# A product in four one-bank PSUM buffers from a common pool, a first attention in groups, and a new order of work

## The chip, the core and the metric

The program runs on one core of a Trainium2 chip. The metric is device time in microseconds (us) of one execution. Before the change three timed runs gave 225.18, 226.84 and 223.76 us, median 225.18. The profile is of one more execution of the same program, which took 223.1 us.

The core has five engines that run side by side, each strictly in its own order: TensorE (PE, matrix products; PEld is the loading of its stationary operand), VectorE (DVE), ScalarE (ACT), GpSimd (POOL) and SyncE (SP), which here issues all DMAs. PE writes its products to PSUM, which these kernels use as eight banks of 512 floats in each of 128 partitions; here DVE and ACT read it, and POOL works on SBUF alone.

## What is computed

```python
# x: 4 batches x 12480 tokens x 128 channels, inducing: 32 x 128, all float32
def mab(q, kv):
    s = scale * (q @ kv.transpose(0, 2, 1))       # scale = 1 / sqrt(128)
    s = s - s.max(-1, keepdims=True)
    a = np.exp(s)
    a /= a.sum(-1, keepdims=True) + 1e-09
    return a @ kv
h = mab(I, x)              # first attention: 32 inducing points look at all tokens of a batch
y = mab(x, h)              # second attention: each token looks at the 32 points
u = y @ w_in               # 128 -> 2048, 49920 tokens in all
out = (u - np.tanh(u)) @ w_out                    # 2048 -> 128
```

## The kernel before, in words

**The algebra.** Every row of `y` is a mean of the 32 rows of `h`. The kernel replaces `u - tanh(u)` by its tangent at the mean of `h`, so the last two products shrink to one small matrix per batch, `P` (32 x 128, with a column of ones). Per token there remain scores against `h`, an exponential and one product with `P`, divided by the sum of the exponentials. `bound` works out whether the tangent is close enough and writes `limit`; a general branch behind it is taken only if not.

**The stages.** Each batch has eight full steps of 1536 tokens and a rest step of 192, nine in all.

- `first(b)`: for each step a load of `xT` (channels on partitions, 768 KB), four matmuls of scores (L341 with `indT_sb`), and on DVE a copy out of PSUM with the maxima (L375). After all nine steps the maximum over the batch goes through PE twice (L384, L392) and becomes the bias `nb` (L394). Then for each step an exponential on ACT (L429), a transpose on DVE (L433) and twelve accumulating matmuls into one bank, `hacc` (L440). These need the tokens on partitions as well: for the steps in `TURNED` PE transposes `xT` (L415, three groups of four) and ACT or DVE moves the result to SBUF (L419); for the others a second copy is loaded (`xn`, L423). Then the sums, the division (L456) and a fold (L458) give `h` (`hT_all`, L460).
- `linear(b)`: `h` through `w_in`, tangent, `w_out`: a chain over PE, ACT, DVE and POOL (L475 to L538), at whose end stands `P_all` of the batch.
- `second(b, s)`: scores (L341 with `hT_all`), the maximum on DVE (L559, L560), the exponential on ACT (L563), and the product with `P` on PE (L570), twelve matmuls into `o_ps`, **one tile of four PSUM banks**, bank `q` for a quarter of the tokens. Then DVE adds a small number to the sums in all four banks at once (L582) and inverts them (L583). The eviction is in three pieces: banks 0 and 1 together, bank 2, bank 3. A piece goes either through DVE, which multiplies on the way out (L604), or through ACT as a plain copy (L608) followed by the multiplication on POOL (L612). Then the store (L619).
- `weight`: the weights come as 64-bit words and are turned into floats on ACT, POOL and DVE (L300 to L323) early in the program.

**The order.** The five engines' orders aren't the text's. `Plan.order` goes through a plan of all operations with a cost each, and whenever an engine is free in that plan it takes the ready operation with the least priority number (`pri`, from the table `K`), if the buffers it needs are free. `STAY` is added to operations that would change PE's kind of tile; `TURNED` says which steps are turned on PE. `PLACES` has the number of buffers of each kind (23 large ones, `big`, for loads and results; four one-bank PSUM buffers `ps` beside `o_ps`), `MOST` limits how many serve one purpose. On the chip each engine then waits by semaphores for what its next instruction needs. The semaphores follow the tiles: where DVE and ACT read the same PSUM tile, the later one in the order waits for the earlier.

## Time and profile before

| | |
|---|---|
| median of three timed runs | 225.18 us |
| the profiled execution's own time | 223.1 us |
| its span, first to last instruction | 221.2 us |
| mean granted PE clock | 0.92 of full |
| busy PE / DVE / ACT / POOL | 165.5 / 154.6 / 106.1 / 92.7 us |
| DMA | 67.23 MB, 304 GB/s over the span |

The profile is one execution. Busy time is the time in which an engine executed something; PE's is modelled, as matmuls overlap. A row of the grouped view has line, engine, operation, tiles and shapes, count, then busy us and mean ns of one, then the idle time just before and what ended it (`<-`). A row of the timeline has the start, the duration and the instruction, merged where the same one repeats.

### The profile page before, as it was taken

To read this page: it belongs to the slowest core of one execution; us is meant where nothing else is said; L and a number is where in the kernel's file an instruction comes from. 1 tells how busy PE (TensorE), PEld (TensorE's weight loads), DVE (VectorE), ACT (ScalarE), POOL (GpSimd) and SP (SyncE) were. 2 spreads that over 40 slices of the span, in tenths; PEclk is the share of its full clock that TensorE was granted. 3 is DMA by queue.
4 is the path that set the end of the run, shared out by engine and by line. 5 is a ranking of instruction groups with operands and counts; after the bars stand their busy time and mean duration, and the time that the engine had idled before them with its cause. 6 is when DMAs were issued, how large, how long until landed. Compare 5 with 4: busy or idle time off the path is not lost.

```text
span 221.2 us, 6573 instructions
## 1 busy us (share of the span) xinstructions
PE 165.5 (75%) x2627; PEld 104.2 (47%) x2627; DVE 154.6 (70%) x456; ACT 106.1 (48%) x226; POOL 92.7 (42%) x103
## 2 busy tenths in 40 slices
PE   0999939878599979599986997999787676364320
PEld 0565727433476635255764544667544433133210
DVE  3367889999957657767984778897656957555350
ACT  2122898436377634447942551696445233443200
POOL 4001189766513437563021563304636734436230
PEclk9999999999589999979999999999999859998555
DMA  6999969999649999997999999999956440655640
GB/s 190 419 423 379 400 221 331 413 424 419 217 142 280 366 393 397 340 387 234 304 391 422 383 410 341 417 407 324 395 217 247 184 162 1 284 215 214 257 190 16
DMA packets 13909, 67.23 MB, mean 304 GB/s; under 512 B 1712, under 2 KB 2864, under 8 KB 13872
## 3 DMA queue, kind: packets, MB, share of 16 engines
q1 hardware_dynamic: 13872, 66.74, 79.0%
q8 instruction: 23, 0.38, 0.7%
q14 instruction: 14, 0.11, 0.2%
HBM read 41.17 MB, written 25.56 MB: 302 GB/s over the span
## 4 chain that ended last, share of the span: by engine, by line
PE 33%; DVE 30%; DMA 14%; ACT 13%; issue 5%; POOL 1%; SPq 0%; DVEq 0%; ACTq 0%
PE ps L341 9%; PE o_ps L570 9%; PE ps L415 9%; ACT big L608 8%; DVE big L604 6%; DMA big<-in_xT 6%; DMA big<-in_xn 5%; PE ps L440 3%; DMA out<-big 3%; DVE mb L559 2%; DVE big L317 2%; DVE s L375 2%; DVE big L306 2%; DVE et L433 2%; ACT ex L563 2%
## 5 line engine op out<-in xcount | busy, mean ns | idle before, releaser
L612 POOL TENSOR_TENSOR big<-big,mb 128x768 f32<-128x768 f32 (+1 forms) x49 | 58.4, 1208 | 76.7 <-ACT big L608 67.3
L570 PE MATMUL o_ps<-P_all,ex 32*128 32x129 f32 (+1 forms) x784 | 34.6, 302 | 22.8 <-DVE big L604 13.2
L608 ACT COPY big<-o_ps 128x768 f32<-128x768 f32 (+1 forms) x49 | 32.5, 668 | 29.0 <-DVE S_all L582 14.5
L570 PEld LDWEIGHTS o_ps<-P_all,ex 32*128 32x128 f32 (+1 forms) x784 | 27.5, 198 | 38.6 <-issue 18.9
L415 PE MATMUL ps<-ident,big 128*128 128x128 f32 x216 | 34.3, 303 | 5.0 <-DVE s L375 3.7
L604 DVE TENSOR_TENSOR big<-o_ps,mb 128x384 f32<-128x384 f32 (+1 forms) x47 | 26.0, 577 | 16.5 <-ACT big L608 16.5
L563 ACT ACTIVATE ex<-ps,mb 128x384 f32<-128x384 f32 (+1 forms) x36 | 20.0, 555 | 36.6 <-DVE mb L560 22.9
L341 PE MATMUL ps<-big,indT_sb 128*32 128x384 f32 x256 | 29.6, 527 | 9.4 <-DMA big<-in_xT 8.6
L419 ACT COPY big<-ps 128x512 f32<-128x512 f32 x33 | 19.0, 585 | 34.3 <-PE ps L415 33.6
L415 PEld LDWEIGHTS ps<-ident,big 128*128 128x128 f32 x216 | 26.3, 154 | 17.1 <-issue 4.9
L440 PE MATMUL ps<-big,et 128*32 128x128 f32 x768 | 27.8, 275 | 5.8 <-DVE et L433 4.4
L341 PE MATMUL ps<-big,hT_all 128*32 128x384 f32 x256 | 28.6, 508 | 2.3 <-DVE W L517 1.7
L440 PEld LDWEIGHTS ps<-big,et 128*32 128x32 f32 x768 | 20.8, 109 | 12.6 <-DVE et L433 6.0
L375 DVE TENSOR_SCALAR_CACHE_REDUCE s<-ps 128x384 f32<-128x384 f32 (+1 forms) x36 | 18.2, 509 | 11.2 <-PE ps L341 11.1
L559 DVE TENSOR_REDUCE mb<-ps 128x1 f32<-128x384 f32 (+1 forms) x36 | 18.3, 509 | 4.2 <-PE ps L341 4.1
L429 ACT ACTIVATE s<-s,nb 128x384 f32<-128x384 f32 (+1 forms) x36 | 20.8, 585 | 0.3 <-DVE nb L394 0.3
L433 DVE STREAM_TRANSPOSE et<-s 128x384 f32<-128x384 f32 (+1 forms) x36 | 18.3, 524 | 1.8 <-PE ps L440 1.2
L419 DVE COPY big<-ps 128x512 f32<-128x512 f32 x21 | 14.2, 686 | 4.2 <-PE ps L415 4.0
L582 DVE TENSOR_SCALAR S_all<-o_ps 128x12 f32<-128x12 f32 (+1 forms) x36 | 5.8, 162 | 14.3 <-PE o_ps L570 13.3
L300 POOL TENSOR_SCALAR big<-big 128x512 f32<-128x512 f32 x8 | 6.4, 809 | 19.3 <-DMA big<-in_w_in 19.3
L341 PEld LDWEIGHTS ps<-big,indT_sb 128*32 128x32 f32 x256 | 6.5, 112 | 16.4 <-issue 11.1
L341 PEld LDWEIGHTS ps<-big,hT_all 128*32 128x32 f32 x256 | 6.9, 110 | 8.8 <-issue 4.3
(115 smaller groups left out, 173.2 us busy)
## 6 DMA issues: line engine op xcount, KB each, us to landing
big<-in_xT SPq DMA_DIRECT2D x32, 768.0 KB, 8.6
out<-big SPq DMA_DIRECT2D x32, 768.0 KB, 5.2
big<-in_xn SPq DMA_DIRECT2D x14, 768.0 KB, 7.8
big<-in_w_in SPq DMA_DIRECT2D x4, 512.0 KB, 12.0
big<-in_w_out SPq DMA_DIRECT2D x4, 512.0 KB, 7.7
xr<-in_xT SPq DMA_DIRECT2D x4, 96.0 KB, 10.7
xnr<-in_xl SPq DMA_DIRECT2D x4, 96.0 KB, 8.0
out<-otr SPq DMA_DIRECT2D x4, 96.0 KB, 2.8
```

Source lines behind the costliest of these rows:

```text
L341: nc.tensor.matmul(ps[q * m:(q + 1) * m, :sg], lhsT=w, rhs=seg(x, nq, None, q), start=True, stop=stop)
L375: nc.vector.tensor_scalar(out=s1.get()[:P, :sg], in0=ps.get()[:P, :sg], scalar1=1.0, scalar2=None, op0=ALU.mult, op1=ALU.max, accum_out=mx ...
L415: nc.tensor.transpose(out=ps.get()[:, k * 128:(k + 1) * 128], in_=xt.get()[:, c:c + 128], identity=ident)
L419: copy(x.get()[:, 4 * g:4 * g + 4, :].rearrange("p k c -> p (k c)"), ps.get())
L433: add("DVE", 0.5 if s < NS else 0.25, lambda et=et, s1=s1s[s], P=P, sg=sg, kb=kb: nc.vector.transpose(out=et.get()[:P, :kb].rearrange("p k ...
L440: nc.tensor.matmul(hacc.get()[q * m:(q + 1) * m, :C], lhsT=et.get()[:P, k, :], rhs=x.get()[:P, k, :], start=(s == 0 and k < NQ), stop=last ...
L559: nc.vector.tensor_reduce(out=mb.get()[:P, 0:1], in_=ps.get()[:P, :sg], axis=AX.X, op=ALU.max)
L563: add("ACT", 0.49 if full else 0.28, lambda: nc.scalar.activation(out=ex.get()[:P, :sg], in_=ps.get()[:P, :sg], func=AF.Exp, bias=mb.get() ...
L570: nc.tensor.matmul(o_ps[:T, q, r * (C + 1):(r + 1) * (C + 1)], lhsT=ex.get()[p, r * T:(r + 1) * T], rhs=P_all[p, b, :], start=True, stop=True)
L604: nc.vector.tensor_tensor(out=dst(), in0=o(q0, q1)[:, :, :, :C], in1=by_q(rs()).unsqueeze(3).to_broadcast([T, q1 - q0, nr, C]), op=ALU.mult)
L608: nc.scalar.copy(out=dst(), in_=o(q0, q1)[:, :, :, :C])
L612: nc.gpsimd.tensor_tensor(out=x, in0=x, in1=rs().unsqueeze(2).to_broadcast([T, w, C]), op=ALU.mult)
```

## The change

It has three parts and a new order.

**The last product.** The tile `o_ps` goes. `second` takes a one-bank buffer for each quarter `q` from the pool `ps`, which now has all eight banks; scores, transposes, `hacc` and the small products use the same pool. The sums are handled by one small DVE instruction per bank (L620, four where L582 was one) and one reciprocal as before (L623). The eviction is in four pieces, one bank each: banks 0 and 1 always through ACT (L636), banks 2 and 3 through ACT or DVE (L632), as the plan finds them free; POOL multiplies banks 0 and 1 in one instruction still (L641), banks 2 and 3 in one each where ACT copied them.

**The first attention.** For batches 0 and 2 the nine steps form three groups, steps 0 to 2, step 3, and steps 4 to 8, each with its own maximum and bias, so a group's exponentials and accumulation need only that group's scores. Each group accumulates into its own third of `hacc`. At the end factors `f` bring the groups to the common maximum (small instructions on DVE and ACT, and two more of 128 x 128 in `collect`). Batches 1 and 3 keep one group. `indT_sb` is scaled once at the start on ACT.

**Turned and loaded steps, and the order.** 15 steps are turned on PE instead of 18, so three more `xn` loads of 768 KB. All numbers of `K`, the limits `MOST` and `STAY` are others, so most instructions stand at other places. The instructions on each engine become, where they change: PE transposes L415 216, now L434 180; DVE L604 47, now L632 27; DVE L582 36, now L620 136; ACT L608 52, now L636 109; ACT moves L419 33, now L438 27; DVE moves L419 21, now L438 18; POOL L612 52, now L641 73.

Three places show the order. PE, in the last steps of batch 3; `ex_…` is one step's exponentials. Before (the product of a step is one row):

```order
L341 MATMUL ps_148<-big_89,hT_all 32x384 x4
L570 MATMUL o_ps<-P_all,ex_629 128x129 x12
L341 MATMUL ps_141<-big_214,hT_all 32x384 x4
L570 MATMUL o_ps<-P_all,ex_640 128x129 x12
L341 MATMUL ps_134<-big_315,hT_all 32x384 x4
L570 MATMUL o_ps<-P_all,ex_614 128x129 x12
```

and after (a step's twelve matmuls go round four banks; the first four of each step are shown):

```order
L340 MATMUL ps_159<-big_376,hT_all 32x384 x4
L608 MATMUL ps_153<-P_all,ex_629 128x129
L608 MATMUL ps_138<-P_all,ex_629 128x129
L608 MATMUL ps_166<-P_all,ex_629 128x129
L608 MATMUL ps_175<-P_all,ex_629 128x129
...
L608 MATMUL ps_131<-P_all,ex_644 128x129
L608 MATMUL ps_145<-P_all,ex_644 128x129
L608 MATMUL ps_124<-P_all,ex_644 128x129
L608 MATMUL ps_159<-P_all,ex_644 128x129
L340 MATMUL ps_153<-big_198,hT_all 32x384 x4
L608 MATMUL ps_138<-P_all,ex_620 128x129
```

Each product used the same four banks as the one ahead of it; now successive products use banks that are partly or wholly others.

PE, at the end of `linear` of batch 3. `P_2188` (`P_2288` after) is the nearly finished `P`, L656 (L694 after) is the first product of `bound`. Before:

```order
L570 MATMUL o_ps<-P_all,ex_640 96x129 x2
L532 MATMUL ps_134<-wout_sb,W_677 32x128 x16
L656 MATMUL ps_148<-big_330,cols 32x128 x2
...
L656 MATMUL ps_148<-big_171,cols 32x128 x2
L536 MATMUL ps_141<-P_2188,foldx 128x128
L341 MATMUL ps_134<-big_233,hT_all 32x384 x4
L570 MATMUL o_ps<-P_all,ex_614 128x129 x12
```

and after:

```order
L608 MATMUL ps_131<-P_all,ex_629 128x129
L608 MATMUL ps_175<-P_all,ex_644 96x129
L608 MATMUL ps_124<-P_all,ex_644 96x129
L573 MATMUL ps_159<-P_2288,foldx 128x128
L340 MATMUL ps_153<-big_275,hT_all 32x384 x4
L694 MATMUL ps_159<-big_116,cols 32x128 x2
...
L694 MATMUL ps_159<-big_362,cols 32x128 x2
L608 MATMUL ps_138<-P_all,ex_620 128x129
```

The last product for `P` stood behind `bound`'s and now stands ahead of it, as do the DVE instructions that `bound` begins with.

PE, in batch 0 of the first attention; `mx` is a maximum on its way through PE, `et` the transposed exponentials. Before:

```order
L384 MATMUL ps_134<-ident,mx 1x128
L415 MATMUL ps_141<-ident,big_214 128x128 x4
L415 MATMUL ps_148<-ident,big_233 128x128 x4
L415 MATMUL ps_127<-ident,big_233 128x128 x4
L392 MATMUL ps_134<-one,mr 32x1 x4
L415 MATMUL ps_141<-ident,big_233 128x128 x4
L440 MATMUL ps_148<-big_146,et_366 32x128 x12
```

and after:

```order
L340 MATMUL ps_138<-big_150,indT_sb 32x384 x4
L389 MATMUL ps_145<-ident,mx 1x128
L434 MATMUL ps_153<-ident,big_150 128x128 x4
L434 MATMUL ps_159<-ident,big_150 128x128 x4
L397 MATMUL ps_166<-one,mr 32x1 x4
L389 MATMUL ps_175<-ident,mx 1x128
L340 MATMUL ps_124<-big_171,indT_sb 32x384 x4
L397 MATMUL ps_131<-one,mr 32x1 x4
L340 MATMUL ps_138<-big_192,indT_sb 32x384 x4
L459 MATMUL ps_145<-big_143,et_243 32x128 x12
```

The first accumulation stood behind the scores of all nine steps; now it stands behind those of six, and behind two passes of a maximum.

```diff
-SWITCH, STAY = 0.18, 27.6
-TURNED = ((0, 1, 2, 3, 4, 5, 6, 7), (1, 2, 6, 7), (0, 3, 7), (0, 3, 4))
+SWITCH, STAY = 0.18, 87.5
+TURNED = ((0, 1, 2, 3, 4, 5, 6, 7), (2, 3, 6), (2, 4, 5), (3,))
+GROUPS = ((0, 3, 4), (0,), (0, 3, 4), (0,))
...
-    ps_o = ctx.enter_context(tc.tile_pool(name="ps_o", bufs=1, space=PSUM))
...
-    o_ps = ps_o.tile([128, NQ, 512], F32, name="o_ps")
-    PLACES = dict(big=23, xr=3, xnr=2, s1=11, et=3, ex=3, otr=2, mb=4, ps=4, W=1)
+    PLACES = dict(big=23, xr=3, xnr=2, s1=11, et=3, ex=3, otr=2, mb=4, ps=8, W=1)
...
-    def misc():
-        return Buf(lambda n: home(ps_p, "ps", n, [128, 512]), "ps")
+    def misc(kind="pm"):
+        return Buf(lambda n: home(ps_p, "ps", n, [128, 512]), "ps", kind)
...
+    add("ACT", 0.2, lambda: nc.scalar.mul(out=indT_sb, in_=indT_sb, mul=SC), writes=[ind_b], pri=-500)
...
-        mx, mr, nb = small("mx", [128, 1]), small("mr", [1, m]), small("nb", [128, 1])
...
+        G = len(GROUPS[b])
+        cut = [*GROUPS[b], NSG]
+        nbs, nmx, f = small("nbs", [128, G]), small("nmx", [128, 1]), small("f", [128, G])
+        p = pri + K["lag2"]
+        nb = []
+        def greatest(g):
+            mx, mr, psx, psy = small("mx", [128, 1]), small("mr", [1, m]), misc(), misc()
+            pg = p + K["step1"] * cut[g + 1] - 400
+            add("DVE", 0.14, lambda: nc.vector.tensor_reduce(out=mx.get(), in_=mxg.get()[:, cut[g]:cut[g + 1]], axis=AX.X, op=ALU.max),
+                reads=[mxg, *mx_parts[cut[g]:cut[g + 1]]], writes=[mx], pri=pg)
+            add("PE", 0.3, lambda: nc.tensor.transpose(out=psx.get()[:1, :128], in_=mx.get(), identity=ident),
+                reads=[mx, ident_b], writes=[psx], pri=pg, mode="f")
+            add("DVE", 0.27, lambda: nc.vector.tensor_reduce(
+                out=mr.get(), in_=psx.get()[:1, :128].rearrange("o (q i) -> o i q", q=NQ), axis=AX.X, op=ALU.max),
+                reads=[psx], writes=[mr], pri=pg)
+            def column():
+                for q in range(NQ):
+                    nc.tensor.matmul(psy.get()[q * m:(q + 1) * m, :1], lhsT=mr.get(), rhs=one, start=True, stop=True)
+            add("PE", 0.3, column, reads=[mr, one_b], writes=[psy], pri=pg, mode="x")
+            nb.append(Buf())
+            add("DVE", 0.15, lambda: nc.vector.tensor_scalar(out=nbs.get()[:, g:g + 1], in0=psy.get()[:, :1], scalar1=-1.0, scalar2=None,
+                                                             op0=ALU.mult), reads=[psy, nbs], writes=[nb[g]], pri=pg)
+        for g in range(G):
+            greatest(g)
+        if G > 1:
+            add("DVE", 0.14, lambda: nc.vector.tensor_reduce(out=nmx.get(), in_=nbs.get(), axis=AX.X, op=ALU.min),
+                reads=[nbs, *nb], writes=[nmx], pri=p - 300)
+            add("ACT", 0.25, lambda: nc.scalar.activation(out=f.get(), in_=nbs.get(), func=AF.Exp, scale=-1.0, bias=nmx.get()),
+                reads=[nmx, nbs, *nb], writes=[f], pri=p - 300)
         hacc = misc()
-        last = {k % NQ: (s, k) for s in range(NSG) for k in range(shape(s)[2])}
+        group = [max(g for g in range(G) if cut[g] <= s) for s in range(NSG)]
+        first_k, last_k = {}, {}
+        for s in range(NSG):
+            for k in range(shape(s)[2]):
+                first_k.setdefault((group[s], k % NQ), (s, k))
+                last_k[group[s], k % NQ] = (s, k)
...
-            q0 = p + 5 + K["step2"] * s
+            g0 = group[s]
+            q0 = p + K["step1"] * cut[g0 + 1] + K["step2"] * (s - cut[g0])
...
-                nc.scalar.activation(out=t, in_=t, func=AF.Exp, scale=SC, bias=nb.get()[:P], accum_out=sums.get()[:P, s:s + 1])
-            add("ACT", 0.6 if s < NS else 0.4, ex, reads=[nb, sums], writes=[s1s[s], part], pri=q0 + K["exp1"])
+                nc.scalar.activation(out=t, in_=t, func=AF.Exp, bias=nbs.get()[:P, g:g + 1], accum_out=sums.get()[:P, s:s + 1])
+            add("ACT", 0.6 if s < NS else 0.4, ex, reads=[nb[g0], nbs, sums], writes=[s1s[s], part], pri=q0 + K["exp1"])
...
-                    nc.tensor.matmul(hacc.get()[q * m:(q + 1) * m, :C], lhsT=et.get()[:P, k, :], rhs=x.get()[:P, k, :],
-                                     start=(s == 0 and k < NQ), stop=last[q] == (s, k))
+                    nc.tensor.matmul(hacc.get()[q * m:(q + 1) * m, g * C:(g + 1) * C], lhsT=et.get()[:P, k, :], rhs=x.get()[:P, k, :],
+                                     start=first_k[g, q] == (s, k), stop=last_k[g, q] == (s, k))
...
+        def total():
+            if G == 1:
+                nc.vector.tensor_reduce(out=sm.get(), in_=sums.get(), axis=AX.X, op=ALU.add)
+                return
+            for g in range(G):
+                nc.vector.tensor_scalar(out=junk.get()[:, cut[g]:cut[g + 1]], in0=sums.get()[:, cut[g]:cut[g + 1]],
+                                        scalar1=f.get()[:, g:g + 1], scalar2=None, op0=ALU.mult, op1=ALU.add,
+                                        accum_out=sg_.get()[:, g:g + 1])
+            nc.vector.tensor_reduce(out=sm.get(), in_=sg_.get(), axis=AX.X, op=ALU.add)
...
+        def collect():
+            nc.vector.tensor_scalar(out=hs.get(), in0=hacc.get()[:, :C], scalar1=(fr.get()[:, :1] if G > 1 else rs.get()), scalar2=None,
+                                    op0=ALU.mult)
+            for g in range(1, G):
+                nc.vector.scalar_tensor_tensor(out=hs.get(), in0=hacc.get()[:, g * C:(g + 1) * C], scalar=fr.get()[:, g:g + 1],
+                                               in1=hs.get(), op0=ALU.mult, op1=ALU.add)
...
+        o_b = [misc(None) for q in range(nq)]
...
-                    nc.tensor.matmul(o_ps[:T, q, r * (C + 1):(r + 1) * (C + 1)], lhsT=ex.get()[p, r * T:(r + 1) * T],
+                    nc.tensor.matmul(o_b[q].get()[:T, r * (C + 1):(r + 1) * (C + 1)], lhsT=ex.get()[p, r * T:(r + 1) * T],
                                      rhs=P_all[p, b, :], start=True, stop=True)
-        add("PE", 0.66 if full else 0.25, product, reads=[ex, P_b[b]], writes=[o_b], pri=pri + K["prod"], mode="r")
+        add("PE", 0.66 if full else 0.25, product, reads=[ex, P_b[b]], writes=o_b, pri=pri + K["prod"], mode="r")
-        def recip():
-            S = sums_all.get()[:T, n0:n0 + n]
-            nc.vector.tensor_scalar(out=by_q(S), in0=o(0, nq)[:, :, :, C], scalar1=1e-9, scalar2=None, op0=ALU.add)
-            nc.vector.reciprocal(out=mb.get()[:T, 2:2 + n], in_=S)
+        def begun():
+            for q in range(nq):
+                nc.vector.tensor_scalar(out=sums_all.get()[:T, n0 + q * nr:n0 + (q + 1) * nr], in0=o(q)[:, :, C], scalar1=1e-9,
+                                        scalar2=None, op0=ALU.add)
+        add("DVE", 0.02 + 0.12 * nq, begun, reads=[sums_all, *o_b], writes=[part], pri=pri + K["rec"])
+        add("DVE", 0.25, lambda: nc.vector.reciprocal(out=mb.get()[:T, 2:2 + n], in_=sums_all.get()[:T, n0:n0 + n]),
+            reads=[part], writes=[mb, part2], pri=pri + K["rec"])
...
-            ways = dict(DVE=(0.08 + 0.133 * w, whole), ACT=(0.05 + 0.1025 * w, plain))
-            one_way = "DVE" if k == 2 else "ACT"
-            done = add(one_way, *ways.pop(one_way), reads=[mb, o_b, ot], writes=[part], pri=pri + K["ev"], **ways)
+        ways = dict(DVE=(0.08 + 0.133 * nr, whole), ACT=(0.06 + 0.1025 * nr, plain))
+        done = []
+        for q in range(nq):
+            piece = Buf()
+            pieces.append(piece)
+            eng = "DVE" if q == 3 else "ACT"
+            cost, f = ways[eng]
+            also = {e: (c, lambda f=f, q=q: f(q)) for e, (c, f) in ways.items() if e != eng and q >= 2}
+            done.append(add(eng, cost, lambda f=f, q=q: f(q), reads=[part, *([mb] if q >= 2 else []), o_b[q], ot], writes=[piece],
+                            pri=pri + K["ev"], **also))
+        for q0, q1 in ((0, 2), (2, 3), (3, 4)) if full else ((0, 2),):
+            add("POOL", 0.15 + 0.215 * (q1 - q0) * nr, lambda q0=q0, q1=q1: norm(q0, q1), reads=[mb, ot], writes=pieces[q0:q1], pri=pri,
+                needed=lambda x=done[q0]: x.eng == "ACT")
```

86 lines of the change are left out of this document (31 added, 55 removed).

## The prediction

> **What bounds the kernel now.** I read the head of the page first, then the busy time by stretches, then the timeline of the last stretch, and last who waits for whom.
>
> ```profile
> span 221.2 us, 6573 instructions
> ...
> PE 165.5 (75%) x2627; PEld 104.2 (47%) x2627; DVE 154.6 (70%) x456; ACT 106.1 (48%) x226; POOL 92.7 (42%) x103
> ```
>
> ```profile
> core 0: us, PE busy (x) PEld busy (x) DVE busy (x) ACT busy (x) POOL busy (x), PEclk, DMA share, GB/s
> 20.00:60.00 40.00, 30.21 (x416) 18.97 (x415) 37.47 (x87) 24.25 (x52) 25.29 (x23) 0.95 0.92 351
> 60.00:160.00 100.00, 89.32 (x1612) 57.93 (x1614) 73.89 (x236) 57.64 (x131) 39.05 (x36) 0.97 0.94 349
> 163.50:181.20 17.70, 11.98 (x184) 7.71 (x188) 13.10 (x41) 7.56 (x17) 11.57 (x12) 0.84 0.47 188
> 181.20:213.50 32.30, 16.26 (x255) 9.46 (x255) 17.33 (x51) 11.38 (x19) 13.93 (x11) 0.82 0.47 186
> ```
>
> No engine is full over the whole span, but the stretches differ. From 20 to 60 DVE is (37.47 of 40 us); from 60 to 160 PE (89 of 100) and the DMA (0.94) nearly are. After 163.5, where the last first attention is done, nothing is: in the last 32.3 us the busiest engine works 54% of the time. Something there is a chain. One turn of it (start, duration, instruction):
>
> ```profile
> 193.56 0.55 DVE L559 TENSOR_REDUCE mb<-ps 128x1 f32<-128x384 f32 x1
> ...
> 193.79 0.95 PE L570 MATMUL o_ps<-P_all,ex 32*128 32x129 f32 x24 [1.48 <-DVE big L604]
> 194.15 0.21 DVE L560 TRANSPOSE_TENSOR_REDUCE mb<-mb 128x1 f32<-128x32 f32 x1
> ...
> 194.47 0.58 ACT L563 ACTIVATE ex<-ps,mb 128x384 f32<-128x384 f32 x1 [1.88 <-DVE mb L560]
> ...
> 194.68 0.85 PE L341 MATMUL ps<-big,hT_all 128*32 128x384 f32 x8
> 194.80 0.17 DVE L582 TENSOR_SCALAR S_all<-o_ps 128x12 f32<-128x12 f32 x1 [0.44 <-PE o_ps L570]
> 195.01 0.80 ACT L608 COPY big<-o_ps 128x768 f32<-128x768 f32 x1
> 195.08 0.23 DVE L583 RECIPROCAL mb<-S_all 128x12 f32<-128x12 f32 x1
> 195.84 1.02 DVE L604 TENSOR_TENSOR big<-o_ps,mb 128x384 f32<-128x384 f32 x2 [0.53 <-ACT big L608]
> 195.88 1.47 POOL L612 TENSOR_TENSOR big<-big,mb 128x768 f32<-128x768 f32 x1 [1.74 <-ACT big L608]
> ```
>
> ```profile
> 197.01 0.95 PE L570 MATMUL o_ps<-P_all,ex 32*128 32x129 f32 x24 [1.48 <-DVE big L604]
> ...
> 203.48 1.68 PE L570 MATMUL o_ps<-P_all,ex 32*128 32x129 f32 x24 [2.02 <-ACT big L608]
> ```
>
> Product, sums, ACT's copy, DVE's two pieces, next product: 197.01 − 193.79 = 3.22 us a step, strictly one after another. DVE could have started when ACT did, at 195.01; it waits for ACT to leave `o_ps`. From 203 on the product takes 1.68 instead of 0.95 us, after a PE wait of 2.02.
>
> ```profile
> DVE big L604 <- ACT big L608: 16.5, 24, 2.9
> ```
>
> That wait of one reader for another costs DVE 16.5 us in 24 places of the program. It comes with the tile of four banks.
>
> The Trainium skill (PSUM — Partial Sum Buffer, PSUM bank collisions raise a hardware error) states that two engines must be kept apart in one bank and quadrant, reads against reads too, while accesses to different banks run clean. The trace shows DVE waiting although its banks aren't those that ACT reads, so by that page the wait is the tile's and one tile per bank ends it; were it the chip's, the first rival's 3.2 us a step would stand.
>
> **The change part by part.** *The loop in the tail.* The prices of its instructions (mean ns after the busy time):
>
> ```profile
> L612 POOL TENSOR_TENSOR big<-big,mb 128x768 f32<-128x768 f32 x29 | 42.6, 1470 | 70.9 <-ACT big L608 61.6 <-DVE et L433 8.3 <-PE ps L341 1.0
> L415 PE MATMUL ps<-ident,big 128*128 128x128 f32 x216 | 34.3, 303 | 5.0 <-DVE s L375 3.7 <-ACT big L419 0.9 <-ACT ex L563 0.3
> ...
> L604 DVE TENSOR_TENSOR big<-o_ps,mb 128x384 f32<-128x384 f32 x44 | 23.4, 553 | 16.5 <-ACT big L608 16.5
> ...
> L608 ACT COPY big<-o_ps 128x768 f32<-128x768 f32 x29 | 23.1, 797 | 17.2 <-DVE S_all L582 14.5 <-DMA out<-big 2.2 <-PE ps L440 0.3
> ...
> L612 POOL TENSOR_TENSOR big<-big,mb 128x384 f32<-128x384 f32 x20 | 16.5, 828 | 5.8 <-ACT big L608 5.8
> ...
> L608 ACT COPY big<-o_ps 128x384 f32<-128x384 f32 x20 | 9.5, 480 | 11.8 <-DVE big L604 10.5 <-PE ps L440 0.7 <-DVE mean_all L499 0.7
> ...
> L582 DVE TENSOR_SCALAR S_all<-o_ps 128x12 f32<-128x12 f32 x32 | 5.3, 165 | 13.3 <-PE o_ps L570 12.4 <-ACT ex L563 0.7
> ...
> L582 DVE TENSOR_SCALAR S_all<-o_ps 96x2 f32<-96x2 f32 x4 | 0.5, 135 | 1.0 <-PE o_ps L570 0.9
> ```
>
> The three-element L620 isn't in the trace. It lies between the 135 ns for two elements and the 165 for twelve; I take 0.14 us, nearer the two. In the usual step now, three pieces go through ACT and one through DVE. PE has 0.95 + 0.85 = 1.80 us of it; DVE 0.55 + 0.21 + 4 x 0.14 + 0.23 + 0.55 = 2.10; ACT 0.58 + 3 x 0.48 = 2.02; POOL 1.47 + 0.83 = 2.30. Where a product takes a bank of the one before it, it waits for product, sum and two copies: 0.95 + 0.14 + 2 x 0.48 = 2.05 and some 0.2 of gaps. So POOL paces, at 2.30; I take 2.4. The tail runs from `P_all` of batch 3 to POOL's last piece:
>
> ```profile
> 163.40 0.54 PE L458 MATMUL ps<-foldx,hs 128*128 128x160 f32 x2
> ```
>
> ```profile
> 175.39 1.83 PE L532 MATMUL ps<-wout_sb,W 128*32 128x128 f32 x32
> ...
> 178.53 1.93 PE L656 MATMUL ps<-big,cols 128*32 128x128 f32 x32 [1.31 <-DVE cols L649]
> ...
> 179.25 0.58 ACT L563 ACTIVATE ex<-ps,mb 128x384 f32<-128x384 f32 x1 [4.30 <-DVE S_all L582]
> ...
> 179.72 0.26 ACT L535 COPY P<-ps 128x128 f32<-128x128 f32 x1
> ...
> 181.23 0.27 ACT L538 COPY P_all<-ps 128x128 f32<-128x128 f32 x1 [0.24 <-PE ps L536]
> ```
>
> ```profile
> 212.90 0.61 POOL L612 TENSOR_TENSOR otr<-otr,mb 96x256 f32<-96x256 f32 x1 [1.07 <-ACT otr L608]
> ```
>
> That is 181.2 to 213.5, 32.3 us, with eight full steps and the rest step in both orders. After: seven turns of 2.4 are 16.8; the last step from product to POOL 0.95 + 0.56 + 1.44 + 0.83 = 3.8; rest step 0.6; I leave 2 for `bound`'s DVE work between. Together 23.2, so **−9**. At the bounds 2.3 a turn with nothing between (−12), and 3.0 (−5), if PE's clock falls as at 203 and a step costs PE nearer 1.68 + 0.85 and more.
>
> *`linear` of batch 3* took 163.4 to 181.2. L532 ended at 177.2, but the next step, the copy L535, ran at 179.72: ACT stood at L563, which waited 4.30 us for DVE, and DVE was at `bound`'s terms until L656 began. These now stand behind. The copy then starts near 177.3, −2.4, and its PE product no longer has L656's 1.93 us ahead. The products in that stretch also go faster; PE's chain instructions stood behind them. I take **−4** (−2 to −5). What is late next is POOL, 11.57 busy of 17.7 and getting about 0.4 us a step more.
>
> *The front, to 163.5.* Off PE go 36 transposes at 34.3 / 216 = 0.159 us, 5.7 us, of which 24 are batch 3's, 3.8 us in the stretch where PE is nearly full. On PE come four passes of a maximum, five short matmuls each; the nearest row is the transpose's 0.303 us for one alone, so 4 to 6 us at worst if exposed, and nothing if, as the order puts it, scores and transposes stand between; they replace waits for steps 4 to 8 in the beginning. Behind a waiting one all of PE is queued, so I keep 2 us of it. On DVE, 36 L582 become 136 L620, 136 x 0.14 − 5.8 = +13; L604 from 47 to 27, 20 x 0.553 = −11; some 26 small ones for the groups at 0.14 to 0.55, say 0.2, +5; three moves and one weight instruction less, at 0.55 to 1 each, −3. About +4 us in 155, spread out, on an engine with 26 us to spare in the middle. ACT gets 109 copies at 0.48 for 52 that took 23.1 + 9.5 and about 1, +18 us, and six moves less at 0.5 or more, so about +15 on 106, POOL 17 x 0.83 + 3 x 1.47 + more weights, about +20 on 93; both are half idle.
>
> The DMA gets three loads of 786 kB, 2.36 MB: at 349 / 0.94 = 371 GB/s, +6.4 us where it is nearly full. But in SP's order 12 full stores stand ahead of the last `xn` load where 17 stood; five times 786 kB less, −10.6 us. So the loads end some 4 us earlier if the DMA sets the pace, and PE with −3.8, fewer waits for `o_ps`, and one product less ahead of the fold (20 for 21) is ready for it. I take **−5**, with −11 if DMA and PE gains add up and +4 if the stores shift back and half of the 6.4 stays.
>
> *Sum.* 221.2 − 5 − 4 − 9 = 203 of span. Around it lay 1.9 us (223.1 − 221.2): 205. The timed median stood 2 above the profiled execution, within a spread of 3, so I forecast 206 for a median.
>
> **The rivals.** *The loop closes again.* Eight banks hold less than two steps with scores, transposes and `hacc` beside them, and DVE and ACT still go one after the other in each bank: 0.95 + 4 x 0.165 + 3 x 0.48 = 3.05 and gaps, 3.2 a step as now. For it: two banks in common in successive products. Against: ACT starts on the first bank while DVE sums the second. Then only the reordering of `bound` (−3) and half of the front (−2) are left: 225 − 5 = 220.
>
> *The loads eat the front.* The 6.4 us of extra loads stay, because PE and DMA were full side by side: 225 + 6 − 13 = 218. For it: 0.94 of the DMA; against: the stores moved behind.
>
> *POOL paces all, slower.* Stores wait for POOL, and SP's one queue puts loads behind waiting stores:
>
> ```profile
> POOL big L612 <- ACT big L608: 67.3, 26, 10.8
> ```
>
> ```profile
> SPq L619 <- POOL big L612: 64.8, 28, 5.9
> ```
>
> ```profile
> L538 ACT COPY P_all<-ps x4: 253/266/268, 66.5 to 181.2; 128x128 f32<-128x128 f32 x4
> ```
>
> From the first `P_all` at 66.5 POOL has 33 steps' worth (32 and four rests). If each costs 2.3 of work and still the wait of today, 67.3 / 33 = 2.0, POOL ends at 66.5 + 33 x 4.3 = 208; the end is 7.7 us behind (221.2 − 213.5): 218. With 4.7 a step, a wait of 2.4 for ACT's longer queue, it is 231. It decides from 4.6. Against: POOL's waits come from the loop that goes.
>
> ```profile
> 30.50 1.52 DVE L317 TENSOR_SCALAR big<-big 128x512 uint32<-128x512 uint32 x1 [0.24 <-POOL big L310]
> ...
> 36.81 0.38 DVE L317 TENSOR_SCALAR big<-big 128x512 uint32<-128x512 uint32 x1
> ```
>
> DVE's work on SBUF alone takes 0.38 to 1.52 us for the same instruction, the longer one beside POOL. The Trainium skill (GPSIMD Engine Reference, Key points) says that POOL shares its SBUF interfaces with VectorE; these rows agree, and by it 20 us more of POOL would slow DVE. The step's DVE instructions read PSUM, though, and L604 means 553 beside a steady POOL, so it adds little to this rival's chance.
>
> **How the numbers follow.** Forecast 0.62, at 206, its own range 198 to 213; loads 0.18 at 218; loop 0.12 at 220; POOL 0.08 at 231 (half of it under 229). The range 197 to 219 leaves out POOL (0.08), half of the loop's cases (0.06) and a tenth of the forecast's at the low end (0.06), and takes in the bounds of tail and front. This kernel's three times spread by 1.4%, so 2% is about what can be told: faster is under 220.7, slower over 229.7. Faster: 0.62 + 0.16 + 0.06 = 0.84; same 0.11; slower 0.05.
>
> **What would show it.** Right: DVE's L632 has no wait for ACT's L636 worth naming; products of the last eight steps follow at 2.2 to 2.6 us; POOL is the busiest engine of the tail; L573 comes within 1.5 us of L569's end; the last fold (L495) is at 152 to 163. Wrong: turns at 3 or more, with PE waiting for ACT at L608 (the loop); the fold after 166 with the DMA share at 0.95 or more until then (loads); stores held by POOL all through the middle, with loads behind them (POOL).

## The result

After the change four runs gave 202.53 to 208.14 us, median 206.51, against 224.88 before (223.76 to 226.84): a ratio of 0.905, 95% interval 0.891 to 0.920, faster. The ratio leaves out the two slower runs of the changed kernel (208.04 and 208.14), whose granted clock was 0.93 where the other two had 0.94; by the medians it is 0.918. In a later series it was 206.02 against 224.60, ratio 0.930 (0.922 to 0.939). The head of the page after:

```profile
span 200.7 us, 6827 instructions
...
PE 158.4 (79%) x2627; PEld 101.6 (51%) x2627; DVE 154.5 (77%) x562; ACT 112.0 (56%) x281; POOL 113.3 (56%) x126
```

The stretches that answer to those of before; the columns are the same (busy us of PE, PEld, DVE, ACT, POOL, PE's clock, DMA share, GB/s):

```profile
core 0: us, PE busy (x) PEld busy (x) DVE busy (x) ACT busy (x) POOL busy (x), PEclk, DMA share, GB/s
60.00:150.00 90.00, 80.97 (x1538) 52.61 (x1538) 69.75 (x281) 56.14 (x153) 47.47 (x47) 0.97 0.97 365
170.00:193.00 23.00, 16.07 (x279) 9.98 (x267) 19.59 (x74) 15.02 (x39) 21.58 (x21) 0.96 0.74 294
```

The tail is now 23 us in which POOL works 94% of the time, where the busiest engine before had 54%. The timeline after, from the last fold to POOL's last piece:

```profile
153.85 0.54 PE L495 MATMUL ps<-foldx,hs 128*128 128x160 f32 x2
...
165.69 1.72 PE L569 MATMUL ps<-wout_sb,W 128*32 128x128 f32 x28
...
168.42 0.49 PE L573 MATMUL ps<-P,foldx 128*128 128x128 f32 x2
168.95 0.27 ACT L575 COPY P_all<-ps 128x128 f32<-128x128 f32 x1 [1.21 <-PE ps L573]
169.51 1.06 PE L694 MATMUL ps<-big,cols 128*32 128x128 f32 x32
170.50 0.95 PE L608 MATMUL ps<-P_all,ex 32*128 32x129 f32 x24
...
174.24 18.52 POOL L641 TENSOR_TENSOR big<-big,mb 128x768 f32<-128x768 f32 x17 [1.36 <-ACT big L636]
...
185.38 1.80 PE L608 MATMUL ps<-P_all,ex 32*128 32x129 f32 x28
...
192.71 0.61 POOL L641 TENSOR_TENSOR otr<-otr,mb 96x256 f32<-96x256 f32 x1
```

| | before | after | difference |
|---|---|---|---|
| start to the last fold | 163.4 | 153.9 | −9.5 |
| last fold to `P_all` of batch 3 | 17.8 | 15.1 | −2.7 |
| `P_all` to POOL's last piece (the tail) | 32.3 | 24.4 | −7.9 |
| that piece to the end of the span | 7.7 | 7.4 | −0.3 |

Executions of one program differ here, mostly in the first row: in six profiled executions of programs that are the same up to the tail, the last fold came between 153.9 and 160.2, the two latest (159.5 and 160.2) at a granted clock of 0.92 to 0.93 over the span, the others at 0.94 to 0.96. So what follows compares lengths within one execution, and I take −6 to −9.5 for that row (153.9 to 157.5 against 163.4).

The first experiments undid one part each, the later ones went for the order and the tail. Where a part is undone the planner makes another order of everything, which belongs to what was measured. Ratios are to the kernel before, run in the same series; distances to the changed kernel are to its 206.5, as it wasn't run beside the first eight of these experiments.

### The profile page after: what moved, and what is told of

Its sections match the earlier page's. It is cut to its first block, busy times and chain, and to the rows that moved or that the text cites. A ratio compares the mean times of both kernels' runs of the same rounds, so it can differ in the third digit from the quotient of the medians.

```text
span 200.7 us, 6827 instructions
## 1 busy us (share of the span) xinstructions
PE 158.4 (79%) x2627; PEld 101.6 (51%) x2627; DVE 154.5 (77%) x562; ACT 112.0 (56%) x281; POOL 113.3 (56%) x126
## 5 line engine op out<-in xcount | busy, mean ns | idle before, releaser
L641 POOL TENSOR_TENSOR big<-big,mb 128x768 f32<-128x768 f32 (+1 forms) x69 | 75.8, 1126 | 46.9 <-ACT big L636 44.4
L636 ACT COPY big<-ps 128x384 f32<-128x384 f32 x101 | 41.9, 490 | 12.1 <-DVE S_all L620 9.0
L608 PE MATMUL ps<-P_all,ex 32*128 32x129 f32 (+1 forms) x784 | 34.9, 290 | 2.1 <-ACT ex L601 1.4
L608 PEld LDWEIGHTS ps<-P_all,ex 32*128 32x128 f32 (+1 forms) x784 | 27.4, 185 | 15.9 <-ACT big L636 5.6
L434 PE MATMUL ps<-ident,big 128*128 128x128 f32 x180 | 25.3, 291 | 2.3 <-DVE s L374 2.3
L438 ACT COPY big<-ps 128x512 f32<-128x512 f32 x27 | 14.9, 586 | 18.3 <-PE ps L434 18.0
L434 PEld LDWEIGHTS ps<-ident,big 128*128 128x128 f32 x180 | 21.0, 148 | 7.8 <-issue 3.9
L448 ACT ACTIVATE s<-s,nbs 128x384 f32<-128x384 f32 (+1 forms) x36 | 21.1, 592 | 6.0 <-DVE nbs L400 6.0
L597 DVE TENSOR_REDUCE mb<-ps 128x1 f32<-128x384 f32 (+1 forms) x36 | 18.2, 507 | 2.7 <-PE ps L340 2.3
L620 DVE TENSOR_SCALAR S_all<-ps 128x3 f32<-128x3 f32 (+1 forms) x136 | 13.6, 154 | 7.7 <-PE ps L608 6.7
L632 DVE TENSOR_TENSOR big<-ps,mb 128x384 f32<-128x384 f32 x27 | 14.6, 541 | 0.2
L438 DVE COPY big<-ps 128x512 f32<-128x512 f32 x18 | 12.1, 686 | 2.2 <-PE ps L434 1.8
```

The costliest lines, as they stand in the source:

```text
L434: nc.tensor.transpose(out=ps.get()[:, k * 128:(k + 1) * 128], in_=xt.get()[:, c:c + 128], identity=ident)
L438: copy(x.get()[:, 4 * g:4 * g + 4, :].rearrange("p k c -> p (k c)"), ps.get())
L448: nc.scalar.activation(out=t, in_=t, func=AF.Exp, bias=nbs.get()[:P, g:g + 1], accum_out=sums.get()[:P, s:s + 1])
L597: nc.vector.tensor_reduce(out=mb.get()[:P, 0:1], in_=ps.get()[:P, :sg], axis=AX.X, op=ALU.max)
L608: nc.tensor.matmul(o_b[q].get()[:T, r * (C + 1):(r + 1) * (C + 1)], lhsT=ex.get()[p, r * T:(r + 1) * T], rhs=P_all[p, b, :], start=True, s ...
L636: nc.scalar.copy(out=slot(q, q + 1), in_=o(q)[:, :, :C])
```

## Experiments: which part brings it

**One tile per bank, alone.** The kernel before, with its numbers, and in place of the tile of four banks four tiles of one, still their own:

```
-    o_ps = ps_o.tile([128, NQ, 512], F32, name="o_ps")
+    o_t = [ps_o.tile([128, 512], F32, name=f"o_ps{q}") for q in range(NQ)]
```

> The kernel before with its own numbers, plan and order; only the tile of four banks becomes four tiles of one bank. So DVE's sums are four small instructions (36 become 136, about +12 us of DVE) and ACT's copies of two banks become two of 0.48 us; nothing else moves. Theory (the waits between the readers belong to the shared tile): DVE's eviction waits for ACT's copy (16.5 us in 24 places before) nearly vanish, and a step of the tail becomes product 0.95, four sums 0.6, reciprocal 0.23, two DVE pieces 1.05 and gaps: 2.9 to 3.0 us instead of 3.22, as the next product still needs DVE's two banks. Time 219 to 222 us beside 225. Rival (what counts is that more than four banks are there, the split alone is worth nothing): the step stays at 3.2 or grows to 3.6 with the added small instructions, time 224 to 229.

216.15 us, ratio 0.966 (0.949 to 0.982), less than the 219 to 222 that I had expected. The last steps on PE in this run (L570 is still the product):

```profile
189.77 2.06 PE L570 MATMUL o_ps<-P_all,ex 32*128 32x129 f32 x24
192.54 0.59 PE L570 MATMUL o_ps<-P_all,ex 32*128 32x129 f32 x4
193.53 0.94 PE L570 MATMUL o_ps<-P_all,ex 32*128 32x129 f32 x20 [0.40 <-DVE big L597]
195.30 1.86 PE L570 MATMUL o_ps<-P_all,ex 32*128 32x129 f32 x24
198.00 2.42 PE L570 MATMUL o_ps<-P_all,ex 32*128 32x129 f32 x24 [0.55 <-ACT big L602]
```

A step takes 2.7 to 2.8 us (192.54 − 189.77, 195.30 − 192.54), where it took 3.22. So DVE's wait for ACT was the tile's: of the 16.5 us before nothing is left among the waits of this run, and DVE starts on banks 2 and 3 (L597 at 195.15) while ACT is still at banks 0 and 1 (L602, 194.78 to 195.63). That is the reading by the Trainium skill (PSUM — Partial Sum Buffer, PSUM bank collisions raise a hardware error), by which different banks may be read at once. What stays is that a product takes the banks of the one ahead of it, hence PE's waits for DVE and ACT.

**The common pool.** The changed kernel, but the product's banks apart from the other four:

```
-ps=8
+ps=4, po=4
```

> The changed kernel with its numbers, but the last product has four one-bank buffers of its own and all other users share the other four, as before; the plan places the instructions anew. Theory (one tile per bank is the main thing, the common pool the lesser): each product waits for the banks of the one before it, so a tail step is product 0.95, a sum, three copies on ACT 1.44 and gaps, 2.5 to 2.7 us instead of POOL's 2.3; the time grows by 3 to 6 us over the changed kernel, 208 to 212. Rival (the common pool is the main thing): steps of 3 us and more in the tail and PE waiting for ACT in the middle too, 214 or more. Third (POOL paces so that banks don't matter): within 2 us of the changed kernel.

214.72 us, ratio 0.963 (0.947 to 0.979), 8 us over the changed kernel. The tail was 30.4 us, but its plan had left more for it: 244 matmuls of the product start behind `P_all` of batch 3, where the changed kernel has 196, two steps less. A step there took 2.38 us (six from 181.49 to 195.75), below the 2.5 to 2.7 expected and close to POOL's 2.30. So a common pool is worth little in the step; the 8 us lie in a fold at 159.7, 5.9 later, and in the two steps more.

**The groups.** One group in every batch:

```
-GROUPS = ((0, 3, 4), (0,), (0, 3, 4), (0,))
+GROUPS = ((0,), (0,), (0,), (0,))
```

> The changed kernel with one group of steps in all batches, so the first accumulation of batches 0 and 2 waits for all nine scores again; same numbers, the plan places the instructions anew. If the groups carry a good part of the front's gain, the folds of batches 0 and 3 come later, 44 or later for the first (40.3 now, 45.1 before) and 157 or later for the last (154.0 now), and the time is 207 to 210. If they carry nothing, since batch 0 is followed by work that is held elsewhere anyway, the last fold stays at 154 plus or minus 1.5 and the time within 2 us of the changed kernel.

219.55 us, ratio 0.977 (0.959 to 0.995), where 207 to 210 was expected: far more lost than the groups' own instructions could explain. The first fold came at 44.6 (40.3 in the changed kernel), the last at 168.7. The granted clock was 0.89 to 0.90 in all four runs, so part of this can be the clock's.

**Two more steps of batch 3 turned on PE, two loads fewer.**

```
-TURNED = (..., (3,))
+TURNED = (..., (3, 5, 7))
```

> The changed kernel with two more steps of batch 3 turned on PE (3, 5, 7 instead of 3), so two loads of 786 kB fewer (4 us of a full DMA) and 24 transposes more (3.8 us of PE) with six more moves on ACT or DVE. If PE sets the pace up to the last fold, the fold comes 2 to 5 us later and the time is 206 to 210; if the DMA does, it comes 2 to 4 us earlier and the time is 200 to 203. My theory is that both are near their bound there and PE a little nearer: 205 to 207.

210.85 us, some 4 over the changed kernel; the last fold came at 157.9, 4.0 later, as expected if PE sets the pace. Taken together these three still say little of the parts: each lost 4 to 13 us, and each had a new plan made from numbers that were found for another program. The numbers themselves had to be tried.

**The structure with the old numbers, and the reverse.** First the changed kernel planned with `K`, `STAY` and `MOST` of before:

```
-SWITCH, STAY = 0.18, 87.5
-MOST = dict(xT=20, xn=24, ot=9, pm=14)
+SWITCH, STAY = 0.18, 27.6
+MOST = dict(xT=18, xn=12, ot=5, pm=14)
 (and K)
```

> The changed code with eight banks, groups and turned steps as changed, but the order planned with the numbers of before (K, STAY, MOST; the lag of the second attention 24.0). Theory A (the order is part of the gain, worth several us, since three other re-planned variants lost 4 to 13 us): last fold at 157 to 163 where the changed kernel has 153.9, time 210 to 216. Rival B (banks and groups carry the gain, the numbers only suit them): last fold within 2 us of 153.9, time 204 to 208.

225.41 us, ratio 1.017 (0.995 to 1.040): nothing is left of the gain, where I had expected 210 to 216. Then the kernel before with the new numbers, and the one with four tiles of its own with them (the same lines of numbers the other way round):

> The kernel before, its four-bank tile, its turned steps and one group per batch, but planned with the numbers of the changed kernel (K, STAY, MOST). Theory A (the numbers carry most of the gain by themselves): time 206 to 216. Theory B (numbers and structure fit only one another; the changed structure with the old numbers gave 225): time 222 to 240, with the four-bank wait of DVE for ACT as before, some 16 us in all.

> The kernel before with its last product in four tiles of one bank of their own, as in the run that changed only this (216.2), but planned with the numbers of the changed kernel. Theory A (numbers help whatever the structure): time 203 to 212. Theory B (they fit only the common pool and the groups): time 216 to 232.

247.87 us against 224.60, a ratio of 1.10, and 239.58, ratio 1.085 (1.071 to 1.098). From the traces of all six:

| structure, numbers | time | last fold | tail | of it, first to last product |
|---|---|---|---|---|
| before, old | 224.9 | 163.4 | 32.3 | 29.3 |
| four tiles, old | 216.2 | 162.5 | 27.8 | 24.7 |
| changed, old | 225.4 | 179.7 | 22.6 | 15.1 |
| before, new | 247.9 | 189.3 | 30.8 | 28.7 |
| four tiles, new | 239.6 | 187.5 | 24.5 | 21.8 |
| changed, new | 206.5 | 153.9 | 24.4 | 16.4 |

All six have the same 196 matmuls of the product behind `P_all`, so the last column can be compared: 29, 22 to 25, 15 to 16 us by structure, under either set of numbers. The front goes with the pair of structure and numbers: alone, neither brings the last fold ahead by more than a microsecond, and a wrong pair costs 16 to 26 us there. In the three wrong pairs PE's granted clock up to the last fold was 0.93 to 0.94, in the other three 0.97 to 0.98, and PE was busy 7 to 11 us longer there than in the kernel before; so the clock can be a part of the 16 to 26, and whether it is cause or effect of the waits isn't shown. With the new numbers and the old tile the step in the tail is the old one to a hundredth of a microsecond:

```profile
214.57 0.95 PE L570 MATMUL o_ps<-P_all,ex 32*128 32x129 f32 x24 [1.60 <-DVE big L604]
...
217.79 0.95 PE L570 MATMUL o_ps<-P_all,ex 32*128 32x129 f32 x24 [1.48 <-DVE big L604]
...
221.00 0.95 PE L570 MATMUL o_ps<-P_all,ex 32*128 32x129 f32 x24 [1.48 <-DVE big L604]
```

What the front waits for shows in SP's queue. In the kernel before, ahead of the last fold:

```profile
141.61 0.33 SPq L619 DMA_DIRECT2D out<-big  x1
143.51 0.33 SPq L619 DMA_DIRECT2D out<-otr  x1
143.93 0.90 SPq L423 DMA_DIRECT2D big<-in_xn  x2
149.43 0.34 SPq L619 DMA_DIRECT2D out<-big  x1
149.87 2.09 SPq L423 DMA_DIRECT2D big<-in_xn  x2
```

In the changed kernel:

```profile
130.61 12.46 SPq L442 DMA_DIRECT2D big<-in_xn  x7
145.51 8.16 SPq L657 DMA_DIRECT2D out<-big  x5
```

Seven loads go out one behind the other, the last at 142.7, and the stores come after. Before, the loads stood behind stores: the ones at 141.61 and 149.43 had waited 6.4 and 4.6 us for DVE's piece of the result (L604), and the last load went out at 151.5. That is 8.8 us, about the 9.5 by which the fold came earlier. In both kernels the accumulation follows the landing. Before, the last large load landed 8.2 us after it went out, at 159.8, and the fold came 3.6 us behind that; in the changed kernel it landed at 150.6, and the fold came 3.3 behind. PE's accumulations at these landings, before and after:

```profile
159.74 1.07 PE L440 MATMUL ps<-big,et 128*32 128x128 f32 x28 [1.17 <-issue]
```

```profile
150.60 0.86 PE L459 MATMUL ps<-big,et 128*32 128x128 f32 x24 [0.69 <-DMA big<-in_xn]
```

PE's waits for loads in the changed kernel, from 130 to 156 us:

```profile
PE ps L459 <- DMA big<-in_xn: 2.7, 3, 1.5
PEld ps L459 <- DMA big<-in_xn: 2.0, 2, 1.1
```

In the changed structure with the old numbers the loads stand between stores again (these waited 8.9 us for POOL and 4.6 for DVE from 159 to 175), and the accumulation ahead of the fold waits for the last, small one:

```profile
162.83 2.75 SPq L657 DMA_DIRECT2D out<-big  x2
165.82 0.33 SPq L657 DMA_DIRECT2D out<-otr  x1
166.24 1.07 SPq L442 DMA_DIRECT2D big<-in_xn  x1
168.03 6.16 SPq L657 DMA_DIRECT2D out<-big  x2
174.42 0.33 SPq L657 DMA_DIRECT2D out<-otr  x1
174.81 1.14 SPq L442 DMA_DIRECT2D xnr<-in_xl  x1
```

```profile
178.54 0.65 PE L459 MATMUL ps<-xnr,et 64*32 64x128 f32 x6 [2.67 <-DMA xnr<-in_xl]
```

This wait is shown in the trace. That SP's order alone makes the 26 us between the two plans is not: the plans differ on every engine, and an order changed on SP alone wasn't tried.

## Experiments: what paces the tail

**POOL with less to do.** The changed kernel, same plan, without POOL's work on the third pieces of batch 3, which stay unnormalised:

```
         def norm(q0, q1):
+            if q0 == 2 and b == B - 1 and s < NS:
+                return
```

> The changed kernel with the same plan; left out is POOL's multiplication of the third piece (128x384, 0.83 us) in the full steps of batch 3 where ACT evicted it, seven instructions, 5.8 us of POOL; those pieces of the output stay unnormalised. Theory A (POOL paces the tail at 2.30 a step): POOL's last piece comes at 188 to 190 where it came at 192.7, paced then by PE and ACT at about 2.1 a step, and DVE's 1x1 instructions at the end are held less long or not at all; span 196 to 198, time 2 to 5 us below the changed kernel's. Rival B (POOL merely trails behind the products, and the end is set by them, by DVE's bound work or by the stores): the span stays within 1 us of 200.7.

201.85 us against 206.5, and a tail of 20.9 us (171.5 to 192.4) instead of 24.4. From the first product to POOL's end it took 19.4 us (from 173.06) instead of 22.8 (170.50 to 193.32). 5.8 us of POOL's work were worth 3.5: POOL paced the tail, and something else does once that is gone; the products, which ran at 2.1 a step ahead of POOL, are the nearest. The span I had expected, 196 to 198, came in one of four runs (196.5; the profiled one has 200.1), because its fold lay at 156.5.

**DVE in place of POOL.** In every second step of batch 3 DVE does the third piece:

```
         def plain(q):
+            if q == 2 and b == B - 1 and s < NS and s % 2:
+                return whole(q)
```

> The changed kernel with the same plan; in steps 1, 3, 5 and 7 of batch 3 the third piece is evicted and normalised by DVE (128x384, 0.55 us) and not by ACT (0.49) and POOL (0.83): POOL 3.3 us less, DVE 2.2 us more in the last 25 us. Theory A (POOL paces the tail, 21.6 busy of 23, DVE has 3 us to spare there): POOL's last piece 1.5 to 3 us earlier, span 198 to 199.5. Rival B (DVE, 19.6 busy of 23, is as near the bound, and each added 0.55 delays the sums that free the banks): products of the last steps 2.3 and more apart, span 200 to 202.

204.21 us, ratio 0.925 (0.910 to 0.941); a tail of 22.0 us, 20.4 from the first product to POOL's end. The span, 202.3, is above the 198 to 199.5 that I had expected, as the fold lay at 157.5. The engines in that tail, in the columns of the table of stretches:

```profile
172.50:195.00 22.50, 17.44 (x295) 10.93 (x289) 19.51 (x87) 14.90 (x38) 18.87 (x17) 0.99 0.83 328
```

POOL and DVE are now even, and DVE is the last: `limit` is ready at 195.4, a microsecond behind POOL's last piece.

**The closing arithmetic.** In the changed kernel one DVE instruction at the very end, on one number, had taken 3.69 us:

```profile
189.47 0.14 DVE L727 TENSOR_REDUCE low<-ps 1x1 f32<-1x4 f32 x1
189.64 3.69 DVE L728 TENSOR_TENSOR low<-low 1x1 f32<-1x1 f32 x1
193.37 0.15 DVE L729 RECIPROCAL low<-low 1x1 f32<-1x1 f32 x1
```

It ends when POOL's unbroken run does (192.71 + 0.61). The edit keeps part of the scratch in PSUM:

```
-            v.tensor_tensor(out=x[:, 0:1], in0=x[:, 0:1], in1=x[:, 2:3], op=ALU.min)
+            v.tensor_tensor(out=x[:, 0:1], in0=p[:, 0:1], in1=x[:, 0:1], op=ALU.min)   # p in PSUM
 (and the others of decide likewise)
```

> The changed kernel with the same plan; the 1x1 arithmetic at the very end (the function decide) keeps its scratch partly in PSUM, so that each two-operand instruction has one operand in PSUM and one in SBUF, with one small instruction more; the result is the same. In the changed kernel the first of them, both operands in SBUF, took 3.69 us, until POOL's unbroken run ended, where 0.15 is usual. Theory A (DVE instructions with all operands in SBUF are held while POOL streams; an operand in PSUM lifts that): each of the instructions takes under 0.45 us and limit is ready near 191.5 where it was 194.3; the end then follows POOL's last piece, span 199.5 to 200.7. Rival B (the instruction waited for something else that ends at 193.3, a store or a semaphore): one instruction of about 3.5 us remains.

203.44 us (200.55 to 205.11), span 200.6. In this run POOL is busy without a break across the arithmetic, and none of it is held:

```profile
174.43 18.53 POOL L641 TENSOR_TENSOR big<-big,mb 128x768 f32<-128x768 f32 x17 [1.25 <-issue]
...
191.14 0.14 DVE L728 TENSOR_TENSOR low<-ps,low 1x1 f32<-1x1 f32 x1
...
192.13 0.14 DVE L735 TENSOR_SCALAR limit<-ps 1x1 f32<-1x1 f32 x1
...
192.92 0.61 POOL L641 TENSOR_TENSOR otr<-otr,mb 96x256 f32<-96x256 f32 x1
```

`limit` was ready 1.3 us ahead of POOL's end, where it had come 1.0 behind it. The span didn't fall: the end follows POOL's last piece by 7.1 us. My theory was too wide on one point: not every instruction with all its operands in SBUF is held. The reciprocals of a step, with one operand, took 0.18 and 0.23 us beside POOL's unbroken run in the changed kernel. Others with one operand are held, as the last section shows.

**Both edits, beside the changed kernel.**

> The changed kernel once more, as the measure for the next one on the same chip: 203 to 208, last fold at 153 to 158.

> The changed kernel with the same plan and two edits: in steps 1, 3, 5 and 7 of batch 3 DVE evicts and normalises the third piece, and the closing 1x1 arithmetic keeps one operand of each two-operand instruction in PSUM. Theory A (POOL paced the tail, and with the second edit limit is ready before POOL's last piece): from P_all of batch 3 to POOL's last piece 21 to 22.5 us where the changed kernel has 24.4, limit ready within 1 us of that last piece or earlier; time 2 to 3 us below the changed kernel's on the same chip. Rival B (the tail is paced by the products whatever POOL does, the shorter tails so far being a matter of the run): 24 us again, the same time.

206.02 us for the changed kernel (204.42 to 208.76) and 204.63 (200.42 to 209.04) with both edits. From the first product to POOL's end it took 20.6 us with them (178.87 to 199.43) and 22.8 without (176.63 to 199.45), as in the runs above. But the whole tail came out at 23.6 against 24.4: in this profile PE needed 3.0 us from `P_all` to the first product instead of 1.5, at half its clock.

```profile
175.80:178.80 3.00, 3.00 (x40) 1.70 (x40) 1.11 (x3) 1.73 (x6) 1.86 (x2) 0.50 0.39 131
```

`limit` came 1 us behind POOL again, since DVE had more to do. The changed kernel's own fold lay at 160.2 here, outside the 153 to 158 expected. So the 2.2 us are there in the stage, and whether the program is faster stays open: 1.4 us in the median is less than the spread.

## Why the prediction was right, and where it wasn't

The forecast was 206 and the range 197 to 219. All signs named for it but one came: L632 has no wait worth naming (0.2 us idle ahead of all 27); POOL is the busiest engine of the tail; L573 starts 1.0 us behind L569's end; the fold is at 153.9, within 152 to 163. The products don't follow at 2.2 to 2.6: they start at 170.50 and 185.38 with six between, 2.13 on average.

- **Tail, −9 forecast, −7.9 measured.** POOL at 2.30 a step was the right pace: 18.52 us of unbroken work for eight steps, and the 0.61. The products run ahead of POOL, at 2.1, so my sign for the pace was badly chosen. The missing microsecond is the lead: from `P_all` to the first product it takes 1.55 us (1.27 before), and the sum of 23.2 began at the product. `bound`'s L694 (1.06 us) stands in it, as the order in the section on the change showed.
- **`linear`, −4 forecast, −2.7 measured.** The part behind L569 went from 4.0 us (177.2 to 181.2) to 1.5, the −2.4 of the sum. Of the 4.30 us that ACT had waited there, some 2.3 were holds by POOL: of `bound`'s terms on DVE, L646 to L648 took 1.45, 0.75 and 0.80 us beside POOL's run from 175.18 to 178.22, and the same three take 0.22, 0.23 and 0.27 now (L684 to L686), the last two with POOL idle. The prediction had read them as plain work. The rest, "the products in that stretch go faster", failed: fold to L569's end is 13.6 us after and 13.8 before. One DVE instruction of the chain to L569 is held longer there by POOL:

```profile
160.12 2.25 POOL L641 TENSOR_TENSOR big<-big,mb 128x768 f32<-128x768 f32 x2 [0.51 <-ACT big L636]
160.38 1.24 DVE L545 TENSOR_TENSOR u<-mean_all 128x16 f32<-128x16 f32 x1
```

  It took 0.26 before, and the instruction behind it 0.75 in both kernels. Work of DVE on SBUF alone was the case that I had dismissed, "the step's DVE instructions read PSUM": true of the steps' large ones, not of `linear` and of `decide`. And of the two rows of L317 that I compared, the shorter one (0.38) stood beside POOL as well (L309, 36.01 to 37.68), so they didn't show what I read in them.
- **Front, −5 forecast, −6 to −9.5 measured.** The mechanism was the one named, fewer stores ahead of the last load (12, where 17 stood); it was under-sized. Its last load goes out 8.8 us earlier, where I had 4: I took a DMA at the same mean rate, but from 60 to 150 it moves 365 GB/s where it moved 348, 1.5 MB or 4 us more in those 90.
- **Busy times.** POOL came as forecast (113.3 for "about +20 on 93"). ACT has 112.0 where 121 was the sum, since copies that follow one another overlap (three in 1.24 us, not 3 x 0.48); DVE has 154.5 where I added 4, for the same reason (four L620 in 0.35 to 0.49, though one measures 0.154).
- **Sum.** The profiled execution took 202.53 where the sum said 205, and the median is 4.0 above it where I allowed one. The forecast met the median with two errors that cancel.

Of the rivals, the closed loop (220) is answered by the steps of 2.13; the run with four tiles shows the half-way case, 2.7. The loads (218) are hidden, but only in this order: with the old numbers the same structure waits for them and takes 225. The third rival's place, loads behind stores that wait for their result, was right, and I gave it to POOL's load instead of to the order: in the kernel before, the stores ahead of the last loads waited longer for DVE (11.0 us from 128 to 152) than for POOL (4.9), and with the old numbers the changed one's waited 8.9 for POOL. What I had left out altogether is that the order could be worth as much as the structure. I read it at three places on PE, and SP's only by a count.

## What to carry over

A wait of one reader for another that comes from the tile and not from the bank goes with one tile per bank, and it shows in the grouped waits as two engines that never touch the same bank; spread over more banks, the next engine in the row, here POOL, takes over the pace. Numbers that steer an order are part of the structure they were found for: a part that is undone under them, or put in without new ones, measures the misfit as well. Where one queue issues loads and stores, look at which stores stand ahead of the last load, and what they wait for, before adding up bytes. And where DVE works on SBUF alone beside a busy POOL, compare its instructions' durations with the same ones where POOL is idle before taking them for work.

## What the runs showed of the hardware

A DVE instruction that works on SBUF alone can be held while POOL streams. With two operands in SBUF one took 3.69 us for a single number and one 1.24 for 16 in each partition, where 0.15 and 0.17 to 0.18 are usual (L731 and L547 with POOL idle). With one operand in PSUM the single number took 0.14 beside a like POOL run, and POOL's own instructions don't get longer (1470 ns before, here as a group of the changed kernel):

```profile
L641 POOL TENSOR_TENSOR big<-big,mb 128x768 f32<-128x768 f32 x32 | 47.0, 1469 | 46.9 <-ACT big L636 44.4 <-DVE mb L598 2.5
```

One operand doesn't always free it. The TENSOR_SCALAR behind L545 has one, `u` in SBUF; here it is in batch 1 with POOL idle, and in batch 3 beside POOL's second instruction, which ends at 162.37:

```profile
87.46 0.17 DVE L546 TENSOR_SCALAR g_all<-u 128x16 f32<-128x16 f32 x1
```

```profile
161.66 0.75 DVE L546 TENSOR_SCALAR g_all<-u 128x16 f32<-128x16 f32 x1
```

In all 14 traces together it stands 56 times: 25 times with POOL idle, each 0.17 to 0.18 us, and 31 times beside POOL, each 0.54 to 1.37, ending within 0.04 us of the end of a POOL instruction.

The Trainium skill (SBUF — State Buffer, Who interferes with whom) states this conflict for two SBUF inputs, and that the loser waits out the whole instruction of the other. The hold of 1.24 us fits, as it ends with the first of POOL's two instructions; the one of 3.69 doesn't, since it spans the last four of them:

```profile
189.71 3.04 POOL L641 TENSOR_TENSOR big<-big,mb 128x384 f32<-128x384 f32 x3
192.71 0.61 POOL L641 TENSOR_TENSOR otr<-otr,mb 96x256 f32<-96x256 f32 x1
```

The usual case is the short one. In the run with the old numbers the same instruction stood beside an unbroken POOL run up to 216.2 and got its turn after one POOL instruction:

```profile
212.11 1.14 DVE L728 TENSOR_TENSOR low<-low 1x1 f32<-1x1 f32 x1
```

So it did with the product's own banks (0.26 us), with one group (0.22) and with two more turned steps (1.09). Only in the changed kernel and in its repetition (2.46 us, across two more POOL instructions) did it wait past the next POOL instructions to the end of the stream. Why it missed its turn there, no run here shows.
